# Gated linear attention with a mixture of experts: bounds and counts behind the turns, clears on ScalarE

## The chip, the cores and the metric

The program runs on one core of a Trainium2 chip. The metric is the device time of one execution in microseconds; of several executions the median is taken. The engines are called as the profile calls them: PE (TensorE; PEld is its loading of weights), DVE (VectorE), ACT (ScalarE), POOL (GpSimd) and SP (SyncE, which issues most DMAs).

## The reference

Inputs are q, k, v, a_re, a_im of shape (4, 8, 768, 48) and the weights of a gated mixture of 8 experts. First comes a linear attention whose state decays by a complex factor a of magnitude at most 0.999 (B = 4 batches, H = 8 heads, D = 48):

```python
mag = np.sqrt(a_re * a_re + a_im * a_im)
scale = np.minimum(mag, 0.999) / (mag + 1e-06)
a_re_n, a_im_n = (a_re * scale, a_im * scale)
for t in range(S):
    ar, ai = (a_re_n[:, :, t, :, None], a_im_n[:, :, t, :, None])
    new_re = ar * S_re - ai * S_im
    new_im = ar * S_im + ai * S_re
    S_re, S_im = (new_re + kv, new_im)      # kv = outer product of k and v at t
    y[:, :, t] = np.einsum('bhd,bhde->bhe', q[:, :, t], S_re)
```

Its output, as 3072 rows x of 384 numbers, goes to the experts. A row goes to the expert e with the largest logit x @ w_gate; the result is gate * sigmoid(x @ w_output_gate)[e] * (relu(x @ w1[e]) @ w2[e]), where gate is the softmax weight of e, w1[e] is 384 by 1024 and w2[e] 1024 by 384.

## The kernel before, in words

The kernel has two stages. The attention takes about the first 260 us and the experts the rest.

**Attention.** The 3072 rows are 24 chunks of 128 rows. A chunk's decays are summed along its rows by matmuls with triangular matrices: the logarithms of magnitudes give real factors, the angles give turns. Keys are multiplied by the inverse factor and queries by the factor, and both by cosine and sine of the turns, so that the recurrence becomes masked products of keys and queries inside a chunk, and a state between chunks.

Chunks are prepared in ten groups, of 1, 1, 2, 2 and then six times 3 chunks (`sizes`, numbered 0 to 9). For each group these steps run, written as Python generators so that they can be interleaved:

- `prep_exp` (L441): logarithm, exponentials and squares on ACT, products on DVE. Its last two steps are on DVE. The *bound* (L475) writes l2, the logarithm of the magnitude bounded by 0.999, which the sums of `decay` read. The *count* (L479) reads the real part ar and counts the elements that the method can take; only a check at the end of the attention reads that number. On a group of 3 chunks each is one instruction of 128x1152.
- `decay` (L493): per chunk a matmul pair (L499, tile cs), the exponentials re and ri of it on ACT (L231), k times ri (L506) and q times re (L507) on DVE.
- `turning` and `turns` (L554, L534): per chunk the angle of the chunk before is added (L530), a matmul pair sums the angles (L540, tile cs), and DVE rounds (L546), subtracts (L547, output ai) and takes the magnitude (L549, output rnd). The next chunk's turn starts from this one's. The tile cs has two PSUM buffers, which decays, turns, `ratios` (L514, which turns the rcs rows with L95) and the gates share.
- `phase` (L579): sine and cosine of the turns on ACT, into the tile trig.

Exponentials and sines need different function sets on ACT, so a group costs two set loads (L225).

`main` (L791) goes over the chunks. For chunk i it emits `turn` of chunk i+1 (L598: products with trig on DVE into kc and qc, L602; eight transposes each on PE, L95; copies kt and qt on ACT, L614), `state` (L618), `score` (L641: products sc on PE, mask on DVE, L649), `values` (L655) and `finish` (L677: transposes and the row store xn) of chunk i-1. `gates` and `chosen` (L701, L708) compute the logits of two chunks: matmuls (L242), a copy ls (L245), a transpose, and a sum (L250) that belongs to `chosen`. `routing` (L722) ranks the rows of each expert from these and enters them in a list in DRAM.

`side` (L840) is the order of a group's preparation and is stepped beside `main`. For groups after the fourth it is: load the exponential set, then `prep_exp` of the next group mixed with `decay` and `turning` of this one, then the sine set, then `phase`. `first_weights` (L930) follows the last group. It allots the experts' first buffers, among them the two tiles rows (128x1536 each) into which an expert's rows will be gathered, clears both with memsets on POOL (L947), starts the loads of the first weights (raw, L196) and splits them into a high part (L210, ACT) and a low part (L211, DVE).

**Order.** What an engine runs is not the order of this code. A scheduler lists the instructions of each engine by data dependences and a priority, which is the place in the code, moved forward by the numbers of the table `URGE` for the steps that it names (a key is a function's name, or the name with its first argument). `after(a, b, ...)` makes a come behind b in that order, without a semaphore. Every engine then runs its list strictly in order.

**Experts.** Eight experts in order of their counts; per expert the matmuls L1231 and L1169 with relu and split on ACT and DVE (L1235, L1236). Nothing in this stage is touched by the change.

## Time and profile before

| what | us |
|---|---|
| median of 3 runs | 516.22 |
| lowest and highest | 514.34, 519.79 |
| the profiled execution's own time | 514.01 |
| its span, first to last instruction | 512.2 |

The profile is of one execution. A line names the engine, the line of the kernel, output<-inputs and the shape. "Busy" is time with an instruction under way. A bracket such as [1.87 <-DVE kc L602] is the idle time of that engine before the instruction and the instruction that ended it; "issue" there means that the profile shows nothing waited for. PEclk is the granted clock of PE as a share of 2.4 GHz. In the view of instructions in order of time, equal neighbours are merged: x8 are eight instructions. Between the span and the execution's own time lie 1.8 us that no instruction fills.

### The profile page before, as it was taken

To read this page: it belongs to the slowest core of one execution; us is meant where nothing else is said; L and a number is where in the kernel's file an instruction comes from. 1 tells how busy PE (TensorE), PEld (TensorE's weight loads), DVE (VectorE), ACT (ScalarE), POOL (GpSimd) and SP (SyncE) were. 2 spreads that over 40 slices of the span, in tenths; PEclk is the share of its full clock that TensorE was granted. 3 is DMA by queue.
4 is the path that set the end of the run, shared out by engine and by line. 5 is a ranking of instruction groups with operands and counts; after the bars stand their busy time and mean duration, and the time that the engine had idled before them with its cause. 6 is when DMAs were issued, how large, how long until landed. Compare 5 with 4: busy or idle time off the path is not lost.

```text
span 512.2 us, 11231 instructions
## 1 busy us (share of the span) xinstructions
PE 485.5 (95%) x4341; PEld 425.2 (83%) x4341; DVE 338.8 (66%) x746; ACT 319.1 (62%) x605; POOL 119.0 (23%) x138
## 2 busy tenths in 40 slices
PE   7897998989999999988999999999999999999991
PEld 7575885857877877877888899999999999999991
DVE  5769999888998999996588455273644536273210
ACT  6888896978989899855734355272644536272320
POOL 4101210020402122223402732324242223020112
PEclk9999999998999999999999999999999999999996
DMA  8964344426261411007452777163361817130001
GB/s 271 301 203 136 116 117 146 127 47 203 55 176 57 105 34 33 32 21 245 136 174 74 191 180 246 48 218 124 120 187 45 283 41 237 59 92 17 21 22 47
DMA packets 46946, 63.83 MB, mean 125 GB/s; under 512 B 11815, under 2 KB 38710, under 8 KB 46884
## 3 DMA queue, kind: packets, MB, share of 16 engines
q1 hardware_dynamic: 38756, 53.61, 34.5%
q0 software_dynamic: 8128, 9.42, 6.7%
q8 instruction: 36, 0.59, 0.5%
q14 instruction: 26, 0.21, 0.1%
HBM read 53.92 MB, written 9.88 MB: 125 GB/s over the span
## 4 chain that ended last, share of the span: by engine, by line
PE 60%; issue 17%; DVE 7%; ACT 6%; DMA 4%; POOL 4%; POOLq 0%; SPq 0%; DVEq 0%; ACTq 0%
PE up L1231 12%; PE acc L1169 11%; PE tr L95 9%; PE sc L648 7%; PE xo L662 4%; PE st L627 3%; PE xo L668 3%; POOL out_dram L1182 3%; PE cs L499 3%; PE cs L540 3%; DMA ai<-in_a_im_dram 2%; ACT t L231 1%; PE tr L242 1%; DMA rows<-xd,sid 1%; PE xt L95 1%
## 5 line engine op out<-in xcount | busy, mean ns | idle before, releaser
L1236 DVE SCALAR_TENSOR_TENSOR hl<-up,hh 128x464 fp32r<-128x464 f32 (+7 forms) x64 | 37.8, 590 | 84.0 <-ACT hh L1235 80.0
L1235 ACT ACTIVATE hh<-up 128x464 fp32r<-128x464 f32 (+7 forms) x64 | 33.2, 518 | 95.0 <-PE up L1231 91.9
L1231 PE MATMUL up<-xh,w1h 128*128 128x464 f32 (+7 forms) x192 | 68.6, 357 | 0.0
L1231 PE MATMUL up<-xl,w1h 128*128 128x464 f32 (+7 forms) x192 | 67.6, 352 | 0.0
L1231 PE MATMUL up<-xh,w1l 128*128 128x464 f32 (+7 forms) x192 | 67.4, 351 | 0.0
L1169 PE MATMUL acc<-hh,w2h 128*128 128x464 f32 (+6 forms) x168 | 61.4, 365 | 0.0
L1182 POOL DMA_INDIRECT out_dram<-y,sid x28 | 31.8, 1134 | 124.9 <-ACT y L1204 121.9
L1169 PE MATMUL acc<-hh,w2l 128*128 128x464 f32 (+6 forms) x168 | 59.2, 352 | 0.0
L1169 PE MATMUL acc<-hl,w2h 128*128 128x464 f32 (+6 forms) x168 | 59.1, 354 | 0.0
L1065 POOL DMA_INDIRECT table<-entry,addr x20 | 27.8, 1388 | 131.9 <-DVE addr L1061 128.0
L648 PE MATMUL sc<-qt,kt 96*128 96x128 f32 x384 | 53.0, 281 | 0.0
L648 PEld LDWEIGHTS sc<-qt,kt 96*128 96x128 f32 x384 | 47.0, 191 | 4.5 <-issue 2.7
L1110 POOL DMA_INDIRECT rows<-xd,sid x28 | 34.7, 1239 | 51.0 <-DVE w2l L211 24.2
L662 PE MATMUL xo<-scores,v 128*48 128x128 f32 x384 | 44.4, 281 | 0.5 <-DVE scores L649 0.5
L668 PE MATMUL xo<-qt,state 96*48 96x128 f32 x320 | 37.9, 275 | 0.0
L1231 PEld LDWEIGHTS up<-xl,w1h 128*128 128x128 f32 x192 | 36.0, 188 | 1.3 <-DVE xl L1026 0.4
L211 DVE TENSOR_TENSOR w1l<-raw,w1h 128x512 fp32r<-128x512 f32 x48 | 30.4, 686 | 9.9 <-ACT w1h L210 9.9
L1231 PEld LDWEIGHTS up<-xh,w1l 128*128 128x128 f32 x192 | 36.1, 188 | 0.9
L1231 PEld LDWEIGHTS up<-xh,w1h 128*128 128x128 f32 x192 | 36.1, 188 | 0.8
L649 DVE TENSOR_TENSOR scores<-sc,mask 128x512 f32<-128x512 f32 x48 | 32.6, 683 | 5.2 <-PE sc L648 4.7
L662 PEld LDWEIGHTS xo<-scores,v 128*48 128x48 f32 x384 | 27.9, 123 | 9.8 <-issue 4.6
L1169 PEld LDWEIGHTS acc<-hh,w2h 128*128 128x128 f32 x168 | 31.6, 188 | 1.0
(211 smaller groups left out, 1090.3 us busy)
## 6 DMA issues: line engine op xcount, KB each, us to landing
raw<-in_moe_w_dram SPq DMA_DIRECT2D x32, 768.0 KB
ar<-in_a_re_dram SPq DMA_DIRECT2D x24, 192.0 KB
ai<-in_a_im_dram SPq DMA_DIRECT2D x24, 192.0 KB
k<-in_k_dram SPq DMA_DIRECT2D x24, 192.0 KB
q<-in_q_dram SPq DMA_DIRECT2D x24, 192.0 KB
v<-in_v_dram SPq DMA_DIRECT2D x24, 192.0 KB
xd<-xn SPq DMA_DIRECT2D x24, 192.0 KB
rows<-xd,sid POOLq DMA_INDIRECT x28
```

The lines of the kernel that those rows point to most:

```text
L95: return nc.tensor.transpose(out=out, in_=in_, identity=ident[p0:p0 + n, p0:p0 + n])
L211: ins = nc.vector.tensor_tensor(out=lo[:, s], in0=raw[:, s], in1=hi[:, s].bitcast(F32), op=ALU.subtract)
L648: nc.tensor.matmul(sp[:, j * P:(j + 1) * P], r["kt"][:D2, h, :], r["qt"][:D2, h, :], start=True, stop=True)
L649: nc.vector.tensor_tensor(out=r["s"][:, 4 * hh:4 * hh + 4, :], in0=sp.rearrange("p (h t) -> p h t", t=P), in1=mask[i % 2].unsqueeze(1).bro ...
L662: nc.tensor.matmul(op[u * DP:u * DP + D, j * P:(j + 1) * P], vt[c][:, h * D:(h + 1) * D], r["s"][:, h, :], start=True, stop=(cc == 0))
L668: nc.tensor.matmul(op[u * DP:u * DP + D, j * P:(j + 1) * P], xs[:D2, h * D:(h + 1) * D], r["qt"][:D2, h, :], start=False, stop=True)
L1110: nc.gpsimd.indirect_dma_start(out=rows[e % 2][:n, i, :], out_offset=None, in_=xd[:known], in_offset=bass.IndirectOffsetOnAxis(ap=ids[:n, ...
L1169: nc.tensor.matmul(accs[kt][:, :cap], w[:, cs], a, start=(ft == 0 and s == 0), stop=(ft == FT - 1 and s == 2))
L1182: ins = nc.gpsimd.indirect_dma_start(out=out, out_offset=bass.IndirectOffsetOnAxis(ap=ids(e)[:n, i:i + 1], axis=0), in_=y[:n, :], in_offse ...
L1231: nc.tensor.matmul(up[:, :cap], w[:, kt, :], x[:, kt, :], start=(m == 0), stop=(m == 3 * KT - 1))
L1235: nc.scalar.activation(out=hh, in_=up[:, :cap], func=AF.Relu)
L1236: nc.vector.scalar_tensor_tensor(out=hl, in0=up[:, :cap], scalar=0.0, in1=hh.bitcast(F32), op0=ALU.max, op1=ALU.subtract)
```

## The change

Five edits, all in the attention:

1. For groups 5 to 9, bound and count are taken out of `prep_exp` into a generator `bound`, which `side` of the group before runs after its `phase`. The bound is ordered behind the last turn (L547) of the group before. From group 4 on the count comes behind its bound; for groups 0 and 1 that was so already.
2. In `decay` the exponential ri, for the keys, is written before re, for the queries. The scheduler then also puts k times ri before q times re.
3. `URGE` has an entry of 40 for `chosen`, the sum of the gates.
4. `URGE` has an entry of 60 for `turn` of chunk 2 alone.
5. The two memsets of rows on POOL become eight multiplications of the constant iota by 0.0 on ACT, 128x384 each, emitted after the first weight loads.

```diff
@@ -405,7 +405,7 @@
             KEEPV = ()
             XTD = 0
             QTD = 0
-            URGE = {"ranked": 150, "routing": 100, ("routing", True): 300, "turning": 30, **UG}
+            URGE = {"ranked": 150, "routing": 100, ("routing", True): 300, "turning": 30, "chosen": 40, ("turn", 2): 60, **UG}
             XN = 0
             L2B = 2
             INIT = 4
@@ -471,16 +471,26 @@
                 nc.vector.scalar_tensor_tensor(out=lnr, in0=lnr, scalar=2.0, in1=t2, op0=ALU.mult, op1=ALU.add)
                 yield
                 function(out=t2, in_=lnr, func=AF.Exp, scale=-0.5, bias=b_eps)
-                d["l2"] = l2 = early.tile([P, NG, HD], F32, name="l2", bufs=L2B)
-                st["bounded"] = nc.vector.scalar_tensor_tensor(
-                    out=l2.rearrange("p c f -> p (c f)")[:, :w], in0=lnr, scalar=2.0 * math.log(0.999), in1=t2, op0=ALU.min, op1=ALU.subtract)
-                yield
-
-                ins = nc.vector.scalar_tensor_tensor(
-                    out=sq, in0=ar, scalar=0.0, in1=sq, op0=ALU.is_gt, op1=ALU.is_gt, accum_out=count[:, g:g + 1])
-                if g < 2:
-                    after(ins, st["bounded"], "bounds first")
-                yield
+
+                def bound():
+                    d["l2"] = l2 = early.tile([P, NG, HD], F32, name="l2", bufs=L2B)
+                    st["bounded"] = nc.vector.scalar_tensor_tensor(
+                        out=l2.rearrange("p c f -> p (c f)")[:, :w], in0=lnr, scalar=2.0 * math.log(0.999), in1=t2, op0=ALU.min, op1=ALU.subtract)
+                    if g > LATE:
+                        after(st["bounded"], st["turned", starts[g] - 1], "turns first")
+                    yield
+
+                    ins = nc.vector.scalar_tensor_tensor(
+                        out=sq, in0=ar, scalar=0.0, in1=sq, op0=ALU.is_gt, op1=ALU.is_gt, accum_out=count[:, g:g + 1])
+                    if not INIT > g > 1:
+                        after(ins, st["bounded"], "bounds first")
+                    yield
+
+                if g > LATE:
+                    d["bound"] = bound()
+                    yield
+                else:
+                    yield from bound()
 
             @urge
             def prep_trig(g):
@@ -501,8 +511,8 @@
                         after(st["summed"], warmed, "clock")
                     re = early.tile([P, HD], F32, name="re")
                     ri = early.tile([P, HD], F32, name="ri")
+                    function(out=ri, in_=lp[:, :HD], func=AF.Exp, scale=-1.0)
                     function(out=re, in_=lp[:, :HD], func=AF.Exp)
-                    function(out=ri, in_=lp[:, :HD], func=AF.Exp, scale=-1.0)
                     nc.vector.tensor_tensor(out=d["k"][c], in0=d["k"][c], in1=ri, op=ALU.mult)
                     nc.vector.tensor_tensor(out=d["q"][c], in0=d["q"][c], in1=re, op=ALU.mult)
                     (nc.gpsimd if g < 2 else nc.sync).dma_start(
@@ -859,6 +869,8 @@
                 if late:
                     yield from prep_trig(g)
                 yield from mix(phase(g), *([prep_trig(g + 1)] if ahead else []))
+                if ahead:
+                    yield from G[g + 1]["bound"]
                 if not more:
                     yield from ratios(g)
 
@@ -944,8 +956,11 @@
                 ready["pool"], ready["set"] = pool, weight_set(pool)
                 for n in range(2):
                     rows[n] = pool.tile([P, NS, HD], F32, name=f"rows{n}")
-                    nc.gpsimd.memset(rows[n], 0.0)
                 pieces = load_pieces(ready["stage"], who[0])
+                for n in range(2):
+                    for i in range(NS):
+                        nc.scalar.mul(rows[n][:, i, :], iota[:, :HD], 0.0)
+                    yield
                 yield from rest()
                 ready["splits"] = split_pieces(pieces, ready["set"], (st["placed"], st["listed"]))
                 for _ in range(3):
```

The counts of instructions on PE, DVE and SP stay; POOL loses two, ACT gains eight. The scheduler's lists move as follows. Line numbers are of each kernel's own file: behind the new code the same line is 10 higher (L547 is L557, L602 is L612), and L475, L479 are L477, L483.

DVE before, around the second and third turn of group 5 (the rows L546, L547, L549 are one turn; l_1559 is the bound of group 6, sq,count its count, kc and qc the next chunk's products):

```order
L547 TENSOR_TENSOR ai<-cs,rnd 128x384
L649 TENSOR_TENSOR scores<-sc,mask_88 128x512
L530 SCALAR_TENSOR_TENSOR ai<-ai,full_turn 32x384
L549 TENSOR_SCALAR rnd<-ai 128x384
L475 SCALAR_TENSOR_TENSOR l_1559<-lnr,t_1232 128x1152
L546 TENSOR_SCALAR rnd<-cs 128x384
L479 SCALAR_TENSOR_TENSOR sq,count<-ar,sq 128x1152
L547 TENSOR_TENSOR ai<-cs,rnd 128x384
L602 TENSOR_TENSOR kc_170<-k,trig 128x768
```

DVE in the changed kernel, from the same third turn on (l_1641 is the bound of group 6):

```order
L556 TENSOR_SCALAR rnd<-cs 128x384
L250 TENSOR_REDUCE logits<-cs 128x32
L557 TENSOR_TENSOR ai<-cs,rnd 128x384
L612 TENSOR_TENSOR kc_170<-k,trig 128x768
L559 TENSOR_SCALAR rnd<-ai 128x384
L659 TENSOR_TENSOR scores<-sc,mask_88 128x512
L612 TENSOR_TENSOR qc_169<-q,trig 128x768
L260 TENSOR_REDUCE mx<-logits 128x4
L477 SCALAR_TENSOR_TENSOR l_1641<-lnr,t_1280 128x1152
L262 TENSOR_TENSOR dl<-logits,mx 128x32
L483 SCALAR_TENSOR_TENSOR sq,count<-ar,sq 128x1152
```

Bound and count have left the third turn's way and stand behind the keys' and queries' products of the next chunk; the sum of the gates (L250) stands ahead of them.

ACT before, at the end of the attention (xt, state, kt and qt are copies out of PSUM, w1h the first weights' high part):

```order
L694 COPY xn<-tr 128x384
L231 ACTIVATE ex<-dl 128x32
L672 COPY xt<-xo 128x512
L231 ACTIVATE en<-los 128x4
L637 COPY state_172<-st 96x384
L614 COPY kt_174<-tr 96x512 x2
L614 COPY qt_173<-tr 96x512 x2
L210 CAST w1h_3376<-raw 128x512 x3
```

ACT in the changed kernel, same place (L962 are the clears):

```order
L231 ACTIVATE ex<-dl 128x32
L682 COPY xt<-xo 128x512
L962 ACTIVATE rows_3384<-iota 128x384 x4
L231 ACTIVATE en<-los 128x4
L962 ACTIVATE rows_3385<-iota 128x384
L647 COPY state_172<-st 96x384
L962 ACTIVATE rows_3385<-iota 128x384 x3
L624 COPY kt_174<-tr 96x512 x2
L210 CAST w1h_3376<-raw 128x512 x2
L624 COPY qt_173<-tr 96x512 x2
```

The eight clears stand between the copies xt and kt, five of them ahead of the state's copy; two of the weights' casts have moved ahead of qt.

## Rows read from the trace of the kernel before

**Rows 1.** The page's first part: busy us (share of the span) and instructions per engine.

```profile
PE 485.5 (95%) x4341; PEld 425.2 (83%) x4341; DVE 338.8 (66%) x746; ACT 319.1 (62%) x605; POOL 119.0 (23%) x138
```

**Rows 2.** By stage: length; busy us PE, PEld, DVE, ACT, POOL; PEclk, DMA share, GB/s.

```profile
60.00:210.00 150.00, 145.16 (x1807) 113.94 (x1805) 137.28 (x325) 130.01 (x237) 23.78 (x19) 0.99 0.35 96
210.00:230.00 20.00, 18.41 (x271) 15.28 (x270) 19.39 (x52) 13.74 (x28) 5.41 (x5) 1.00 0.07 22
230.00:262.00 32.00, 29.35 (x377) 25.11 (x372) 21.01 (x71) 17.55 (x37) 9.60 (x8) 1.00 0.57 174
```

**Rows 3.** Instructions of PE in order of time, 105 to 120 us: start, length; [idle before].

```profile
105.63 0.91 PE L540 MATMUL cs<-ai,tri_t 128*128 128x384 f32 x2
...
114.01 0.19 PE L95 MATMUL cs<-ident,rcs 24*96 24x24 f32 x1 [2.15 <-issue]
114.58 1.41 PE L499 MATMUL cs<-l,tri_l 128*128 128x384 f32 x2 [0.38 <-ACT rc L520]
115.78 1.92 PE L95 MATMUL tr<-ident,kc 128*96 128x128 f32 x8
...
119.31 1.08 PE L95 MATMUL tr<-ident,qc 128*96 128x128 f32 x8
```

**Rows 4.** Instructions of DVE in order of time, 109 to 121 us.

```profile
109.42 0.62 DVE L530 SCALAR_TENSOR_TENSOR ai<-ai,full_turn 32x384 f32<-32x384 f32 x1
...
110.34 1.35 DVE L475 SCALAR_TENSOR_TENSOR l<-lnr,t 128x1152 f32<-128x1152 f32 x1
...
112.08 1.35 DVE L479 SCALAR_TENSOR_TENSOR sq<-ar,sq 128x1152 f32<-128x1152 f32 x1
...
113.35 0.55 DVE L547 TENSOR_TENSOR ai<-cs,rnd 128x384 f32<-128x384 f32 x1
113.82 0.95 DVE L602 TENSOR_TENSOR kc<-k,trig 128x768 f32<-128x768 f32 x1
...
120.49 0.96 DVE L602 TENSOR_TENSOR qc<-q,trig 128x768 f32<-128x768 f32 x1 [1.86 <-PE tr L95]
```

**Rows 5.** PE by stretches of 2 us: busy, granted clock, DMA share, GB/s.

```profile
112.00:114.00 2.00, 0.00 (x0) 1.00 0.00 0
114.00:116.00 2.00, 1.61 (x5) 0.72 0.68 214
116.00:118.00 2.00, 2.00 (x12) 0.50 0.91 243
```

**Rows 6.** GpSimd (POOL), 217 to 221 us, in order of time.

```profile
217.55 2.72 POOL L947 MEMSET rows<- 128x1536 f32 x2
```

**Rows 7.** DVE, ACT and PE, 216 to 225 us, in order of time, a view each.

```profile
217.33 3.15 DVE L549 TENSOR_SCALAR rnd<-ai 128x384 int32<-128x384 int32 x1
...
224.02 0.35 DVE L549 TENSOR_SCALAR rnd<-ai 128x384 int32<-128x384 int32 x1
...
220.52 0.61 ACT L231 ACTIVATE trig<-rnd,b_cos 128x384 f32<-128x384 f32 x1 [2.75 <-DVE rnd L549]
...
221.19 0.91 PE L540 MATMUL cs<-ai,tri_t 128*128 128x384 f32 x2 [1.59 <-DVE ai L530]
```

**Rows 8.** Groups by line and shape: count | busy us, mean ns | idle before.

```profile
L694 ACT COPY xn<-tr 128x384 f32<-128x384 f32 x24 | 11.5, 480 | 4.5 <-PE tr L95 3.1 <-DVE mx L260 0.7 <-DVE q L689 0.6
```

**Rows 9.** Instructions of ACT in order of time, 230 to 237 us.

```profile
230.54 0.59 ACT L672 COPY xt<-xo 128x512 f32<-128x512 f32 x1 [0.90 <-PE xo L668]
...
232.67 0.47 ACT L637 COPY state<-st 96x384 f32<-96x384 f32 x1 [1.18 <-DVE rank L279]
233.60 1.06 ACT L614 COPY kt<-tr 96x512 f32<-96x512 f32 x2 [0.46 <-PE tr L95]
```

**Rows 10.** ACT's waits, 24 to 262 us: us in total, times, longest.

```profile
ACT trig L231 <- DVE ai L547: 4.4, 4, 1.4
```

**Rows 11.** PE and DVE, 42 to 46 us, in order of time, a view each.

```profile
44.59 1.05 PE L95 MATMUL tr<-ident,kc 128*96 128x128 f32 x8 [1.87 <-DVE kc L602]
...
43.03 0.55 DVE L506 TENSOR_TENSOR k<-k,ri 128x384 f32<-128x384 f32 x1
```

## The prediction

> **What bounds the kernel now.** I read the busy shares first, then the table by stage, then PE's own idle times in order of time, then what DVE and ACT did at each of them, and last the ends of the attention on ACT.
>
> PE has work under way for 95% of the span [rows 1]. That share hides two different halves. In the experts the change touches nothing. In the attention PE, DVE and ACT are all nearly full: from 60 to 210 us DVE is busy for 137.28 of 150 us, ACT for 130.01, PE for 145.16 [rows 2]. The PE figure is flattered, because matmuls are counted until their modelled ends. DVE has 12.72 us without work in that stretch, and that is about all that a better order can give there. From 230 us on DVE and ACT have room (21.01 and 17.55 of 32 us), and PE sets the pace [rows 2]. Whatever the attention ends earlier, the experts start earlier, as they need the last chunks before their first matmul.
>
> Two places stand out where PE stops and the instructions that the change moves are the reason.
>
> *The stop at 112 us.* PE idles 2.15 us, then 0.38 us [rows 3]. It is short of a free cs buffer and of keys: the third turn's subtraction, which frees the buffer, ends at 113.90, and the next keys' product starts only at 113.82 [rows 4]. Ahead of both stand the bound and the count of the next group, 1.35 us each [rows 4]. After the stop PE's granted clock is 0.72 and then 0.50, that is the 1.2 GHz level, where it had been 1.00 [rows 5]; the engine did nothing from 112 to 114 us before it fell. Eight transposes then take 1.92 us and a matmul pair 1.41 us, where at full clock the same forms take 1.08 and 0.91 [rows 3]. DVE works without a gap from 109.42 us until it waits 1.86 us for those slow transposes [rows 4].
>
> *The stop at 220 us.* POOL's two memsets run from 217.55 to 220.27 us [rows 6]. The small DVE operation that starts at 217.33 takes 3.15 us, where the same one takes 0.35 us six microseconds later [rows 7]. ACT waits 2.75 us for it, and PE 1.59 us for what follows it [rows 7].
>
> **The change part by part.** All terms are made against the profiled execution's own 514.01 us (512.2 us of span and 1.8 around it). It lies 2.2 us below the median of 516.22, so I add 2.2 us at the end.
>
> *Memsets off POOL.* The DVE operation shrinks from 3.15 to 0.35 us: 2.80 us of DVE, which is the upper end. PE lost 1.59 us, which is the lower end, since PE had other work until then. Between the two I take the middle, -2.2 us. The Trainium skill (SBUF — State Buffer, "Who interferes with whom") says that VectorE and GpSimd share a pair of ports, held by one of them for a whole instruction while the other is fully blocked. The rows agree: the blocked operation ended 0.2 us after the memsets. By that rule the whole 2.8 us would come back to DVE; by PE's own row only 1.59 us would reach the end.
>
> *Clears on ACT.* Eight pieces of 128x384. A copy of that shape takes 0.48 us on ACT [rows 8], the nearest row, though it reads PSUM; eight are 3.8 us. They stand between the copy xt at 230.54 and the copies kt at 233.60. ACT idles 0.90, 1.18 and 0.46 us in that stretch [rows 9], and the last two, 1.64 us, lie behind xt. So kt comes 3.8 - 1.6 = 2.2 us later if all of it is exposed, and nothing later if the earlier queries' products have already moved the queue ahead. What is queued behind: state, kt, qt, and with them PE's transposes, which need the tr buffers that kt empties; also two weight casts that now stand ahead of qt and would hold it if the weights were late. PE has gaps of its own later in that stretch, so I take +0.8 us; ends 0 and +2.2.
>
> *Bound and count behind the turns.* At the stop at 112 us the two instructions no longer stand ahead of the third turn and the keys. The most that can come back is the stop, 2.15 + 0.38 = 2.53 us, and the slow clock, (1.41 - 0.91) + (1.92 - 1.08) = 1.34 us: 3.87 us. The least is nothing: DVE must still do the same 2.7 us somewhere, and it was without a gap. What it lost for certain is its own wait of 1.86 us for slow transposes; I take -1.9 us, the value nearest to that row. At the other boundaries the same pair stands ahead of a second turn, and ACT waits 4.4 us in four places for turns, 112 us among them [rows 10]; PE did not stop there. Bounds -4.4 and, if one boundary starves as 112 us did, +3.9; I take -1.0 us. This holds the unknown effect of all the other moves too, the gates' earlier sum among them.
>
> What the delay of the bound costs: decays of the next group begin after it. The bound of group 6 ran at 110.34 and moves back past a few DVE instructions, to behind the products of the first chunk; its own keys are used only three chunks later, and 24 chunks in the 262 us of the attention are some 11 us each, an estimate from the stages [rows 2]. So nothing there. The count frees its ar buffer as much later, and SP's loads of later groups, which now stand further back in SP's queue, keep two groups' distance. I cost both at nothing.
>
> *Keys first.* It matters where the keys' product is awaited: at 44.59 us PE has idled 1.87 us for kc, and two multiplications of the second chunk (0.55 us each) stood ahead of it [rows 11]. They now stand behind, and the entry for `turn` of chunk 2 lifts the same product. At most -1.1 us; the second chunk is later by as much, so at least 0; I take -0.5 us.
>
> Sum: -2.2 + 0.8 - 1.9 - 1.0 - 0.5 = -4.8 us. 514.0 - 4.8 = 509.2 us, and with the 2.2 us to the median 511.4 us. All ends to one side give -12.2 and +4.5 us, or 504.0 and 520.7 us.
>
> **The rivals.**
>
> *DVE is the limit, the pair only changes place.* For it: DVE runs without a gap around 112 us, and 2.7 us of work remain at each boundary. Against it: DVE has 12.72 us of gaps from 60 to 210, some of them waits for PE and ACT that the stops cause. Then only DVE's own saving counts, -2.8, and the clears, +0.8: 514.2 us.
>
> *The gaps close.* For it: ACT's waits on turns at every boundary. If half of DVE's 12.72 us goes, that is -6.4 in place of the -2.9 for the bounds: -2.2 + 0.8 - 6.4 - 0.5 = -8.3, or 507.9 us. Against it: three engines above 85% busy in strict order seldom fit so well.
>
> *Slower: the stop moves on to the next chunk.* The pair now stands behind the first queries' product of a new group and ahead of the second keys' product. If PE runs dry there, the price per boundary is that of the stop at 112 us with its slow clock, 3.87 us. There are five boundaries. With one such stop the kernel stands at -2.2 + 0.8 - 0.5 + 3.9 = +2.0, or 518.2 us; with two at 522.1 us. It decides from the point where PE's stock of work is less than the 2.7 us of the pair. Against it: in the new order a mask (L659) and the first chunk's kc and qc come before the pair, and the eight transposes on each of these are 1.08 us at full clock [rows 3], some 2.2 us of stock beside the scores.
>
> *The change does not do what it says* is not a rival of weight: the lists show the pair and the memsets moved.
>
> **How the numbers follow.** The forecast has 0.50, the DVE limit 0.27, the closed gaps 0.13, the moved stop 0.10. A measurement of this kernel tells about 1% (5.2 us) from no change, so faster begins at 511.1 us and slower at 521.4 us. The forecast lies almost on the first line; I count half of its chance as faster (0.25), all of the closed gaps (0.13) and 0.02 of the DVE limit: 0.40. Slower is the moved stop with two boundaries or more, and what I cannot see: 0.07. The rest, 0.53, is within 1%. The range of 8 in 10 runs from 505.0, which holds part of the closed gaps, to 517.5, which holds the DVE limit and most of one moved stop.
>
> **What would show it.** Right: L559 never above 1 us; no PE idle above 1 us and granted clock 1.00 where group 5 turns; kc of the third group-of-three starting right behind its sine; clears of about 0.5 us each, kt waiting for no more than 2 us; the attention's last chunk 4 to 6 us earlier. Wrong: a PE idle above 2 us at another boundary with the clock at 0.50 behind it; ACT standing in a weight cast while qt is due; or DVE's gaps from 60 to 210 us still near 12.7 us, with only 2 to 3 us gained, which would be the DVE limit.

## The result and the profile after

The changed kernel takes 519.29 us (median of 12 executions, 518.35 to 523.17), the kernel before 515.57 on the same chip (12 executions, 513.59 to 519.79). The ratio is 1.0084, interval 1.0057 to 1.0111. It is slower by 0.84%, some 4 us, inside the 1% that I took as not told apart from no change, but on the other side of the forecast and above the range of 505.0 to 517.5. The profiled execution took 520.22 us, with a span of 518.4.

From the first `up` matmul of the experts to the end, the two profiles take 248.4 us (before) and 247.5 us (after). In these two profiles everything that was lost was lost in the attention: its last matmul of xo starts at 253.5 us before and at 260.7 after.

The page of the kernel after, first part (answers to [rows 1]):

```profile
PE 490.3 (95%) x4341; PEld 426.3 (82%) x4341; DVE 336.1 (65%) x746; ACT 322.5 (62%) x613; POOL 112.2 (22%) x136
```

The same engine by stage and, at the end of the attention, by 4 us (columns as in [rows 2]):

```profile
60.00:210.00 150.00, 142.03 (x1783) 111.50 (x1782) 131.25 (x308) 126.93 (x229) 19.84 (x19) 0.99 0.34 96
210.00:230.00 20.00, 19.81 (x254) 15.20 (x254) 17.08 (x47) 13.28 (x29) 2.31 (x3) 1.00 0.09 31
230.00:262.00 32.00, 29.00 (x376) 23.65 (x378) 22.81 (x76) 24.56 (x53) 9.46 (x8) 0.95 0.54 158
...
248.00:252.00 4.00, 2.21 (x13) 1.42 (x14) 3.96 (x10) 2.73 (x7) 0.00 (x0) 0.86 0.63 147
252.00:256.00 4.00, 4.00 (x38) 3.20 (x38) 1.46 (x10) 2.90 (x6) 1.07 (x1) 0.72 0.52 117
```

Against [rows 2], every engine does less from 60 to 210 us: DVE 131.25 us where it was 137.28, with 308 instructions for 325. I had hoped that DVE's gaps would close. They grew, from 12.72 to 18.75 us. The clock is not the reason, since PE's granted share is 0.99 in both.

The two stalls that I had aimed at are gone. PE of the kernel after, in order of time, where [rows 3] had the stop:

```profile
111.00 1.83 PE L658 MATMUL sc<-qt,kt 96*128 96x128 f32 x14
113.46 0.91 PE L550 MATMUL cs<-ai,tri_t 128*128 128x384 f32 x2 [0.63 <-DVE ai L540]
...
116.55 1.08 PE L95 MATMUL tr<-ident,kc 128*96 128x128 f32 x8 [0.68 <-DVE kc L612]
...
249.79 0.64 PE L95 MATMUL tr<-ident,kc 128*96 128x128 f32 x4 [2.40 <-ACT xn L704]
```

The stop of 2.15 us at 112 us is gone, and what is left are waits of 0.63 and 0.68 us. But one of the signs that I had named for being wrong is there too, one boundary earlier. PE of the kernel after, and the stretch behind it (columns as in [rows 2]):

```profile
83.50 1.57 PE L550 MATMUL cs<-ai,tri_t 128*128 128x384 f32 x2 [2.01 <-DVE ai L540]
84.00:86.00 2.00, 2.00 (x8) 1.22 (x7) 1.34 (x3) 0.04 (x1) 0.00 (x0) 0.50 0.22 48
```

PE idles 2.01 us and its granted clock is 0.50 behind that. In the profile before, the idle time at this place is 1.43 us. It is 2.0 to 2.1 us in every profile with all of edit 1, and 0.9 to 1.4 us in all others.

The small DVE operation that the memsets had held for 3.15 us [rows 7], in the group by tile rnd, 205 to 232 us (count of instructions, min/median/max ns, first and last start):

```profile
L559 DVE TENSOR_SCALAR rnd<-ai x2: 353/355/357, 216.5 to 228.2; 128x384 int32<-128x384 int32 x2
```

This stall went, but not by edit 5 alone. Run k2 is the changed kernel with the memsets left on POOL. There they run in order of time, beside a DVE product, as

```profile
223.13 2.73 POOL L959 MEMSET rows<- 128x1536 f32 x2
225.10 0.96 DVE L612 TENSOR_TENSOR kc<-k,trig 128x768 f32<-128x768 f32 x1 [2.05 <-ACT trig L231]
```

and the small operation is at its ordinary length from 205 to 240 us:

```profile
L559 DVE TENSOR_SCALAR rnd<-ai x3: 338/350/353, 216.7 to 232.3; 128x384 int32<-128x384 int32 x3
```

With the other edits in, the bound's move among them, it no longer falls beside the memsets (in e2, the move alone, it still does in part and takes 1.70 us), and the product that does takes the same 0.96 us as elsewhere. So here the memsets held nothing that edit 5 could give back.

The clears and what follows them, ACT of the kernel after in order of time (answers to [rows 9]):

```profile
235.99 0.57 ACT L682 COPY xt<-xo 128x512 f32<-128x512 f32 x1
236.46 1.76 ACT L962 ACTIVATE rows<-iota 128x384 f32<-128x384 f32 x4
...
238.22 0.51 ACT L962 ACTIVATE rows<-iota 128x384 f32<-128x384 f32 x1
...
238.99 1.35 ACT L962 ACTIVATE rows<-iota 128x384 f32<-128x384 f32 x3
240.25 1.05 ACT L624 COPY kt<-tr 96x512 f32<-96x512 f32 x2
...
249.25 0.48 ACT L704 COPY xn<-tr 128x384 f32<-128x384 f32 x1 [3.03 <-DVE q L699]
```

The eight clears are 1.76 + 0.51 + 1.35 = 3.6 us, as costed (3.8), and ACT has no gap around them. kt starts 4.26 us behind xt; in k2, without clears, 2.13 us. So the clears hold kt back by 2.1 us, my upper end of 2.2. Ten microseconds later PE stops for 2.40 us for xn (its row above), ACT having waited 3.03 us for DVE. There DVE was late too, in order of time:

```profile
247.00 0.56 DVE L646 TENSOR_TENSOR st<-st,rc 96x384 f32<-96x384 f32 x1 [3.49 <-PE sc L658]
...
248.67 0.55 DVE L699 TENSOR_TENSOR q<-tr,k 128x384 fp32r<-128x384 f32 x1
```

PE's last product for st (L637) had ended at 244.61; DVE starts 2.4 us after it and 0.2 us after PE has worked off the scores that follow (246.81). This lateness is told in the last section. The clock falls behind the stop, to 0.86 and 0.72 in the stretches of 4 us above.

### The profile page after: what moved, and what is told of

Read it like the earlier page. It is cut to its first block, busy times and chain, and to the rows that moved or that the text cites. A ratio compares the mean times of both kernels' runs of the same rounds, so it can differ in the third digit from the quotient of the medians.

```text
span 518.4 us, 11246 instructions
## 1 busy us (share of the span) xinstructions
PE 490.3 (95%) x4341; PEld 426.3 (82%) x4341; DVE 336.1 (65%) x746; ACT 322.5 (62%) x613; POOL 112.2 (22%) x136
## 4 chain that ended last, share of the span: by engine, by line
PE 65%; issue 16%; DVE 6%; ACT 6%; POOL 3%; DMA 1%; POOLq 0%; SPq 0%; DVEq 0%; ACTq 0%
PE up L1246 12%; PE acc L1184 12%; PE tr L95 10%; PE sc L658 7%; PE xo L672 4%; PE xo L678 4%; PE cs L550 3%; PE st L637 3%; POOL out_dram L1197 3%; PE cs L509 3%; PE tr L242 1%; PE xt L95 1%; PE yp L95 1%; ACT t L231 1%; PE tr L902 1%
## 5 line engine op out<-in xcount | busy, mean ns | idle before, releaser
L1080 POOL DMA_INDIRECT table<-entry,addr x20 | 24.5, 1224 | 131.7 <-DVE addr L1076 114.1
L678 PE MATMUL xo<-qt,state 96*48 96x128 f32 x320 | 40.5, 276 | 0.0
L659 DVE TENSOR_TENSOR scores<-sc,mask 128x512 f32<-128x512 f32 x48 | 32.8, 684 | 8.2 <-PE sc L658 7.9
L95 PE MATMUL tr<-ident,kc 128*96 128x128 f32 x192 | 27.7, 287 | 6.2 <-DVE kc L612 3.6
```

The costliest lines, as they stand in the source:

```text
L95: return nc.tensor.transpose(out=out, in_=in_, identity=ident[p0:p0 + n, p0:p0 + n])
L659: nc.vector.tensor_tensor(out=r["s"][:, 4 * hh:4 * hh + 4, :], in0=sp.rearrange("p (h t) -> p h t", t=P), in1=mask[i % 2].unsqueeze(1).bro ...
L678: nc.tensor.matmul(op[u * DP:u * DP + D, j * P:(j + 1) * P], xs[:D2, h * D:(h + 1) * D], r["qt"][:D2, h, :], start=False, stop=True)
```

## The experiments

Ratios are to the kernel before, timed on the same chip, with the 95% interval; 12 executions each where nothing else is said. Four chips were used: one for the runs e, a second for f, a third for a, g, h and k, a fourth for p. All kernels compute everything. The diffs show the lines that tell a run from its neighbours, not whole edits.

### Each edit alone, and each taken out

Edit 5 alone, 1 alone, 3 alone, 2 alone, in this order:

```diff
# e1_clears: only
-                    nc.gpsimd.memset(rows[n], 0.0)
+                        nc.scalar.mul(rows[n][:, i, :], iota[:, :HD], 0.0)
# e2_bound: only
+                    yield from G[g + 1]["bound"]
# e4_chosen: only
+ "chosen": 40
# e3_keys: only ri ahead of re
```

> The kernel before with edit 5 alone: the rows are cleared by eight ACT multiplications, not by two POOL memsets. Theory A (the moved bound costs the time) and theory B (the gates' earlier sum costs it) expect the same here: the 3.15 us DVE operation beside the memsets shrinks to 0.35 us, the eight clears cost ACT some 3.4 us where it has room, and the time is 1 to 2 us below before (513.5 to 514.5 against 515.6 us). Theory C (the clears hold ACT at the end of the attention, where the changed kernel's PE idles 2.40 us at 249.79 us and its clock falls) expects 2 to 4 us above before.

> The kernel before with edit 1 alone: bound and count of groups 5 to 9 behind the turns of the group before. Theory A (the moved bound lets DVE reach the next group late, and DVE then waits for PE): 4 to 7 us above before, some 520 to 522 us, with keys' products 8 to 13 us later from the third group of three on, and DVE waiting 5 us or more for turns' sums. Theory B (the gates' sum): no more than 1 us from before, or 2 us below, as the stop at 112 us goes. Theory C (the clears): 2 us below.

> The kernel before with edit 3 alone: the gates' sum has a priority of 40. Theory B (the sum stands ahead of keys' products on DVE and waits there for PE's logits, so the strictly ordered DVE stands still): 3 to 5 us above before, 519 to 521 us. Theory A (the moved bound) and theory C (the clears): within 1 us of before, 514.6 to 516.6 us.

> The kernel before with edit 2 alone: ri and k times ri ahead of re and q times re. My forecast's term was -0.5 us (0 to -1.1): 514.5 to 515.6 us. Theories A, B and C all expect no loss here; if it is 2 us or more above before, the order of keys and queries is itself the cause, as queries' factors come late in every group.

Measured: clears 1.0036 (1.0005 to 1.0067); bound 1.0011 (0.9979 to 1.0043); gates' sum 0.9999 (0.9965 to 1.0033); keys 0.9995 (0.9961 to 1.0029). Only the clears show anything, and that a loss, near the lower end of what theory C asked for (0.36% is some 1.9 us). Theory A is not met by e2, nor B by e4. None of the four alone makes the 0.84%; edit 4 alone was not run.

Then the changed kernel with one edit undone: 1, 3, 5 and 4.

```diff
# f2_nobound: bound and count back in prep_exp
-                    yield from G[g + 1]["bound"]
# f4_nochosen
- "chosen": 40
# f1_noclears
+                    nc.gpsimd.memset(rows[n], 0.0)
-                        nc.scalar.mul(rows[n][:, i, :], iota[:, :HD], 0.0)
# f5_noturn2
- ("turn", 2): 60
```

> The changed kernel with edit 1 undone (bound and count where they were), the four other edits kept. Alone, edits 1, 2, 3 and 5 moved the kernel by no more than 2 us, so the 4 to 5 us of the whole lie in edits that act together, or in edit 4. Theory D (the moved bound and the gates' earlier sum together: both put DVE work that waits for PE ahead of the next keys' products): 513 to 515.5 us, the loss is gone. Theory E (edit 4, the entry for the turn of chunk 2) and theory F (keys first together with the rest): 518 us or more, as here.

> The changed kernel with edit 3 undone (no entry for the gates' sum), the four other edits kept. Theory D (moved bound and gates' sum together): 514 to 516.5 us, and keys' products no more than some 5 us later than before. If only the moved bound matters beside the clears: 518 us or more. Theory E (edit 4): 518 us or more.

> The changed kernel with edit 5 undone (memsets on POOL again). The chunk's second mask in the changed kernel is already 2.0 us late at 217 us, before the clears run, and 4.8 us late at 246 us. Theory D: 517 to 519.5 us, within 2 us of the changed kernel. Theory C (clears at the end of the attention, with the fall of PE's clock at 250 us): 514.5 to 516 us.

> The changed kernel with edit 4 undone (no entry for the turn of chunk 2). It moves four instructions on DVE and seven on PE near 45 us. Theory D: 518.5 to 520 us, the loss stays. Theory E (edit 4 starts a delay near 45 us that lasts): 514 to 516 us.

Measured: without the bound's move 0.9956 (0.9927 to 0.9986), now faster than before; without the gates' entry 1.0055 (1.0023 to 1.0086); without the clears 0.9992 (0.9956 to 1.0028); without the entry for chunk 2 1.0093 (1.0052 to 1.0135, 8 executions). The loss goes with the bound or with the clears, and stays without edits 3 or 4. Theory D is met by f5 and, in kind, by f2, and missed by f1 and f4; E is not met.

### Which of the two, and in what company

Edits 2 to 4 alone; the clears written earlier, where the memsets stood; and the changed kernel twice more on this chip.

```diff
# g2_keys_gates: edits 2, 3, 4 only
# g1_early: in the changed kernel
                     rows[n] = pool.tile([P, NS, HD], F32, name=f"rows{n}")
+                    for i in range(NS):
+                        nc.scalar.mul(rows[n][:, i, :], iota[:, :HD], 0.0)
                 pieces = load_pieces(ready["stage"], who[0])
```

> The changed kernel once more, for a second profile of the same program. Up to its ACT clears at 236 us it runs the same lists as the run without clears, and yet in the first profile it was 5.6 us behind that run by 228 us, 1.3 of them from a fall of PE's clock at 22 us. Theory G (chance: this lag is of the execution, not of the program): the lag by 228 us is within 2 us here, and the loss comes behind 236 us. Theory H (the lag belongs to the program): 4 to 6 us again.

> As the run before, a third profile of the changed kernel. Theory G expects a lag by 228 us that differs from the first profile's 5.6 us by 2 us or more; theory H 4 to 6 us again.

> The changed kernel with the eight clears still on ACT but emitted at the place of the old memsets, ahead of the first weight loads, so that they stand in two blocks of four ahead of the state's copy, and the copies kt, the casts and the state products behind them stand otherwise. Theory I (not the clears' 3.6 us, but the order that the scheduler makes around them costs: DVE then waits 3.49 us for the state's products and holds the splits behind it): 514 to 516 us. Theory C (the clears' own time on ACT): 518 us or more, as before the edit.

> The kernel before with edits 2, 3 and 4 alone: keys first, the gates' sum and the turn of chunk 2 earlier, with the memsets on POOL and the bound where it was. With the clears beside them these edits gave 512.5 us against 513.9 of before. If the clears gain about 2 us where the bound is not moved (the forecast's memset term): 514 to 515 us here. If the clears cost there too, as they did alone (515.6 against 514.5 us): 510.5 to 512 us.

Measured: edits 2 to 4 alone 0.9945 (0.9914 to 0.9977). Early clears 1.0031 (0.9994 to 1.0067), an interval that touches no change; their 516.90 us lies between theories I and C, so their place wasn't settled. The two single executions of the changed kernel, a1 and a2, took 523.66 and 519.47 us; what parts them is in the last section. By 228 us both lie 4.5 us behind f1 (second mask of the chunk, with the first masks set equal), as theory H had it. But k2, which is f1's own program on this chip, lies 4.6 us behind it: the lag is not of the clears, and goes with the chip.

With edits 2 to 4 in, there are now four cases: neither other edit 0.9945, clears only 0.9956 (f2), bound only 0.9992 (f1), both 1.0084 (after). They come from different chips, so two of them were timed again on the chip of g2, beside two variants of the bound.

```diff
# k1_after: the changed kernel; k2_noclears: f1 again
# h1_count: edits 2 to 4; the bound stays, the count alone goes behind the turns
+                    if g > LATE:
+                        after(ins, st["turned", starts[g] - 1], "turns first")
# h2_six: edits 2 to 4; edit 1 for group 6 only
-                    if g > LATE:
+                    if g == 6:
```

> The changed kernel, timed beside the next three on one chip. Theory J (the moved bound and the ACT clears cost together): 518.5 to 520.5 us, and 4 us or more above the same kernel without clears. Theory K (chance and chips: the two were timed on different chips): within 2 us of it.

> The changed kernel with edit 5 undone, once more, on the chip of the run before. Theory J: 513.5 to 515.5 us. Theory K: 518 us or more where the changed kernel stands at 519 to 520. If PE's signals come late here too (as they did in the profiles of the kernel before and the changed one, by 1 to 2.5 us at some ten places, and in no profile of this kernel so far), the lateness belongs to the chip and not to the program.

> Edits 2, 3 and 4, and of edit 1 the count alone: the count of groups 5 to 9 goes behind the turns, the bound stays where it was; memsets on POOL. With no part of edit 1 this stood at 512.5 us (0.55% below before). Theory L (the delay of the bound, on which the next group's sums wait, is what edit 1 costs): the count alone costs nothing and the stop at 112 us shrinks, 511 to 512.5 us. Theory M (any 1.35 us instruction behind the turns pushes keys' products back): 513.5 us or more.

> Edits 2, 3 and 4, and edit 1 for group 6 alone, whose bound stood ahead of the turn in the stop at 112 us; memsets on POOL. If the gain at the stop is real and the later boundaries give it back: 510.5 to 512 us, and the chunks behind 115 us 2 us or more earlier than with no part of edit 1. If the loss follows from one moved pair alone: 513.5 us or more.

Measured: both 1.0067 (1.0031 to 1.0102); bound only 1.0036 (1.0001 to 1.0072); the count alone 0.9959 (0.9921 to 0.9996); one group 1.0001 (0.9970 to 1.0033). So on one chip 0.9945 goes to 1.0036 by the move of the bound, and to 1.0067 by the clears on top. On this chip the move of the bound is the larger part, 0.91%, with intervals that do not meet, and the clears 0.31%, which alone would be within the intervals. On f1's chip the shares lie the other way: f1, with the move and no clears, is at 0.9992, and f5, with both and without edit 4, at 1.0093. k1 stands where theory J had it; k2's 516.92 us lies between J and K. h2 is in the range of a loss from one moved pair alone.

Where the bound costs it is read from g2 and k1. Start of the second mask on DVE (L649, L659) in nine of the chunks, us:

```
g2      101.64 115.37 124.67 140.88 160.27 177.79 194.86 213.38 249.58
k1      101.58 113.72 122.22 143.01 161.08 182.50 200.37 218.88 255.57
k1-g2    -0.06  -1.65  -2.45  +2.13  +0.81  +4.71  +5.51  +5.50  +5.99
```

The changed kernel gains 2.45 us by 125 us, where the stop was, and gives back 4.6 us by 141 and, after a small gain, 3.9 more by 178. The first clear runs at 233 us, so the +5.50 at 213 us is without any. The experts' first matmul follows: 262.16 in g2, 267.88 in k1.

The same is seen on f1's chip. Up to 217 us f1 and f2 differ in edit 1 alone:

```
f2      102.03 115.54 126.47 142.69 162.07 179.43 196.50 215.02
f1      103.25 114.49 122.98 141.66 159.83 180.76 197.96 216.56
f1-f2    +1.22  -1.05  -3.49  -1.03  -2.24  +1.33  +1.46  +1.54
```

The gain at the stop is given back here too, and more: 5.0 us from 125 to 216 us, against 8.0 us from g2 to k1. (In these two profiles f1 has lost some 1.2 us to a slow clock at 82 to 86 us and f2 some 1.6 us at 115 to 120.)

Why: the bounds of the five groups and the keys' products, by line, 60 to 230 us. First g2 (count of instructions, min/median/max ns, first and last start):

```profile
L475 DVE SCALAR_TENSOR_TENSOR l<-lnr,t x5: 1334/1357/1368, 75.3 to 188.1; 128x1152 f32<-128x1152 f32 x5
...
L602 DVE TENSOR_TENSOR kc<-k,trig x19: 925/951/959, 63.0 to 229.3; 128x768 f32<-128x768 f32 x19
```

and k1:

```profile
L477 DVE SCALAR_TENSOR_TENSOR l<-lnr,t x5: 1344/1347/1349, 88.7 to 202.2; 128x1152 f32<-128x1152 f32 x5
...
L612 DVE TENSOR_TENSOR kc<-k,trig x17: 945/948/959, 63.1 to 221.9; 128x768 f32<-128x768 f32 x17
```

The first bound runs 13.4 us later, the last 14.1 (some 5 us of this last are the lag that k1 has by then), and by 230 us DVE has made two keys' products fewer. How the delay comes about is seen where the next bound, of group 7, stands. DVE of g2 in order of time:

```profile
134.26 1.36 DVE L475 SCALAR_TENSOR_TENSOR l<-lnr,t 128x1152 f32<-128x1152 f32 x1 [0.24 <-ACT t L231]
135.54 0.55 DVE L546 TENSOR_SCALAR rnd<-cs 128x384 f32<-128x384 f32 x1
...
140.41 0.56 DVE L546 TENSOR_SCALAR rnd<-cs 128x384 f32<-128x384 f32 x1
```

and of k1:

```profile
140.83 0.55 DVE L556 TENSOR_SCALAR rnd<-cs 128x384 f32<-128x384 f32 x1
141.67 0.96 DVE L612 TENSOR_TENSOR kc<-k,trig 128x768 f32<-128x768 f32 x1 [0.30 <-ACT trig L231]
...
143.88 0.95 DVE L612 TENSOR_TENSOR qc<-q,trig 128x768 f32<-128x768 f32 x1
144.75 1.35 DVE L477 SCALAR_TENSOR_TENSOR l<-lnr,t 128x1152 f32<-128x1152 f32 x1
146.09 1.35 DVE L483 SCALAR_TENSOR_TENSOR sq<-ar,sq 128x1152 f32<-128x1152 f32 x1
...
149.40 0.95 DVE L612 TENSOR_TENSOR kc<-k,trig 128x768 f32<-128x768 f32 x1
```

Here the bound stood ahead of two turns, not one, and now waits for both and for the products of the next chunk; the pair itself stands ahead of the second chunk's keys. The keys of the second chunk start at 149.40, where g2 has them at 144.01; those of the third chunks of groups 6, 7 and 8 start 8.3, 9.5 and 13.3 us later (146.55 to 154.82, 173.82 to 183.30, 200.66 to 213.92). In g2 they ran 9 to 12 us ahead of the first mask of the chunk before; in k1 2 to 7. DVE had lost its stock of work and waits, by its waits of 60 to 230 us (us in total, times, longest). First g2:

```profile
DVE kc L602 <- ACT trig L231: 1.9, 3, 0.7
DVE rnd L546 <- PE cs L540: 1.7, 4, 0.6
DVE scores L649 <- PE sc L648: 1.4, 4, 0.5
```

and k1:

```profile
DVE rnd L556 <- PE cs L550: 5.5, 4, 2.0
DVE scores L659 <- PE sc L658: 4.9, 6, 2.4
DVE kc L612 <- ACT trig L231: 3.3, 4, 2.1
```

The three sum to 5.0 and 13.7 us; on f1's chip to 6.5 in f2 and 12.6 in f1. The 2.4 us among them, at 140 us, is in part of another kind, told in the last section: in f1 the same mask waits 0.6 us.

h1 takes the rival that any work put behind the turns costs as much. It moves half of the pair, the count, and its profile ends the attention 0.6 us ahead of g2 (last xo 256.05 against 251.70, less a start that was 4.94 us later). If each half cost the same, 0.9990 was due; 0.9959 was measured, and 0.9990 lies just inside the interval. Its 514.47 us lies in the range of theory M; its distance of 0.14% from g2 speaks for L. In its profile the stop at 112 us is gone too; its masks are 1.4 us ahead of g2's at 115 us and 2.0 us behind at 195 (starts set equal). So a count behind the turns gives back some of its gain as well, and whether the late bound or the displaced products cost the time was not separated. h2 shows the exchange at one boundary: its profile gains 5 us against g2 by 115 us and has lost it and 3.5 us more by 150, with a new stop and a slow clock behind it. One moved pair costs 0.56% against g2, more than half of what five cost. PE of h2 by stretches of 4 us:

```profile
144.00:148.00 4.00, 2.31 (x11) 1.27 (x11) 4.00 (x7) 3.66 (x8) 0.00 (x0) 0.91 0.36 65
148.00:152.00 4.00, 4.00 (x34) 2.77 (x32) 3.43 (x8) 1.88 (x4) 0.00 (x0) 0.66 0.09 30
```

### What starts the experts

The best variant, g2, and the changed kernel, each with the fourth load of first weights behind the loads of the routing's lists on SP.

```diff
-                pieces = load_pieces(ready["stage"], who[0])
+                pieces = load_pieces(ready["stage"], who[0], 0, 3)
                 yield from rest()
+                pieces += load_pieces(ready["stage"], who[0], 3)
```

> Edits 2, 3 and 4 (512.5 us, 0.55% below before) with the fourth of the first weights' loads put behind the loads of the lists on SP. Theory N (the experts start 17.1 us after the first list has become row numbers on DVE, sid, in every profile of that chip; the list waits for the scatters into the table, and these land late beside the 0.75 MB weight load): sid 2 to 4 us earlier, 1 to 3 us less in time, 509.5 to 511.5 us, as then the last chunk sets the start. Theory O (the end of the attention on PE sets the experts' start, as the forecast had it): within 1 us of 512.5, or slower, as the late load holds ACT's casts.

> The whole change, with the fourth weight load behind the loads of the lists. In its profiles this load went out at 248.2 us, just ahead of the lists at 248.8, and sid came 4.9 us after the lists went out, where it takes 1.6 to 2.0 us without such a load beside it. Theory N: sid 3 us earlier or more, 515.5 to 517.5 us, so that about half of the 4 us of loss at the seam is this collision. Theory O: 519 us as before.

Measured: 0.9935 (0.9904 to 0.9966) and 1.0072 (1.0035 to 1.0108). The list's numbers came about 2.4 us sooner than in g2 and k1 (starts set equal), the experts' first matmul at most 0.8 us. In these profiles it follows the last xo by 10 to 10.5 us, as in before and after: the last chunk on PE sets it there, not the chain of the lists, and theory O is met. (The 17.1 us of the expectation are 18.5 in k2.) p1, 512.18 us, has the lowest ratio of all; against g2 the 0.1% is not told apart.

That holds for twelve of the profiles. In the eight of the chips of e and f the first matmul follows the last xo by 12.1 to 16.0 us, and PE waits 1.3 to 3.1 us for gathered rows; in none of the twelve does it wait for them. PE of f5:

```profile
261.80 3.40 PE L1030 MATMUL sc<-ident,rows 116*128 116x116 f32 x14 [3.09 <-DMA rows<-xd,sid]
```

There the gathered rows set the start, and part of what edits cost is paid at them: f5's last xo is 0.7 us behind f1's (starts set equal), its first matmul of the experts 3.2 us. The later weight load was not run on those chips.

## Why the prediction was wrong

*The delay of the bound: the step that failed.* I wrote that the bound "moves back past a few DVE instructions" and that "its own keys are used only three chunks later", and costed the delay at nothing. I had read it at one boundary, 112 us, where it stood ahead of one turn and moves by 4.8 us (110.5 in g2, 115.3 in k1). At the other four it stood further ahead and moves by 10.5 to 14 us. Three chunks later was true of the first use, but the keys of the third chunks lost 4 to 7 us of the 9 to 12 that they had been ahead. "Other boundaries", -1.0, became some +8 on the chip of g2 and k1 (from -2.45 at 125 us to +5.50 at 213) and +5 on f1's. That the move costs is shown by g2 and k2; that it does so through the lost lead of DVE fits the rows, but the late bound and the pair's own 2.7 us were not told apart.

*The rival "the stop moves on to the next chunk"* (chance 0.10) comes nearest, and its number by luck: 3.87 us forecast per boundary, 4.6 and 3.9 measured at the two that cost most, and +3.7 us for the whole, between one such boundary (+2.0) and two (+5.9). Its price was a stop of PE with the clock at 0.50 behind it. At a boundary such a stop came only at 83 us, in the profile after; k1, with the same stop and its clock at 1.00, had lost nothing to g2 by 102. At the dear boundaries PE of k1 idles at most 1.07 us, the granted clock is 1.00 from 125 to 220 us, and about 2 us of the 4.6 are the lateness of the last section.

*The stop at 112 us*: it went, and the size is right, -2.45 against -1.9. The term was luck: I had taken DVE's wait for slow transposes, and in g2, whose clock stayed at 1.00 there, that wait does not exist. How the 2.45 us divide was not shown.

*Memsets off POOL and clears on ACT*: the stall went (3.15 to 0.36 us), but -2.2 + 0.8 became a loss: +0.36% alone, +0.1% without the bound's move (f2 against g2, two chips), +0.31% with it (k1 against k2). Here I added two terms, the move of the bound and the memsets, that remove the same stall. Without the move, the 1.59 us of PE did come back: between the same two masks, at some 197 and 225 us, e3 (with memsets) takes 28.4 us and e1 (with clears) 26.8. Why e1 is still slower was not shown; against e3 its profile shows no loss behind 195 us. With the move and edits 2 to 4 there was no stall left to take away (k1 and k2 both take 29.7 us between these masks), and the clears, which met no idle ACT as at my upper end of +2.2, were all cost. The stop of 2.40 us is in five profiles with both edits (after, a1, a2, k1, p2), and in all five DVE starts the state product 2.3 to 2.4 us after PE has ended it. In f5, with both edits (but not edit 4) on f1's chip, DVE starts 0.1 us after, and PE has no stop above 0.9 us there; nor has g1, with the clears earlier. So the lateness has its part in that stop; how the two edits lead up to it wasn't shown.

*Keys first and the gates' sum*: each alone nothing (-0.5 forecast). Together with edit 4 they give -0.55%, if the bound stays. Which of them carries it wasn't separated, and the parts were timed on another chip than g2. I had put the gates' earlier sum into the unknown effect of "all the other moves"; alone it has none.

By the steps on one chip: -0.55% (edits 2 to 4), +0.91% (bound), +0.31% (clears) make +0.67%, some 3.5 us; I had -0.9% in all.

## What to carry to other kernels

An instruction that starts a later group's preparation is not idle baggage in front of a stall: ask at each boundary where it goes, and what the engine would have worked ahead with. Before two gains are added, ask whether one edit already removes what the other is to remove: here the moved bound took the DVE operation away from the memsets. A stop that is taken away at one place is worth its length only if the lead of the engines behind it stays, so follow a chunk's start to the end of the stage before a gain is counted. And an edit's worth hangs on the others and on the chip: the parts alone, on one chip, gave nothing or little; on another all five gave +0.67%, and three of them without the rest -0.55%.

## What the runs showed of the hardware

**The same program waits at other places on another chip.** f1 and k2 are one program, 0.9992 on one chip and 1.0036 on the other. ACT of f1 in order of time:

```profile
136.90 1.28 ACT L225 ACT_TABLE_LOAD   x1
138.19 0.58 ACT L682 COPY xt<-xo 128x512 f32<-128x512 f32 x1
```

PE of f1:

```profile
137.60 0.48 PE L678 MATMUL xo<-qt,state 96*48 96x128 f32 x3
```

ACT of k2:

```profile
137.70 1.28 ACT L225 ACT_TABLE_LOAD   x1
141.65 0.59 ACT L682 COPY xt<-xo 128x512 f32<-128x512 f32 x1 [2.67 <-PE sc L658]
```

PE of k2:

```profile
138.39 0.48 PE L678 MATMUL xo<-qt,state 96*48 96x128 f32 x3
...
140.45 1.05 PE L658 MATMUL sc<-qt,kt 96*128 96x128 f32 x8
142.53 0.43 PE L672 MATMUL xo<-scores,v 128*48 128x128 f32 x4 [1.03 <-ACT xt L682]
```

In f1 the copy xt starts 0.1 us after the last xo ends (138.08). In k2 it starts 2.8 us after (138.87), when PE has worked off its scores, and PE then waits for it. The same 2.7 to 2.8 us stand there in the profiles of k1, after, a1, a2, g1 and p2, and at most 0.3 in the other profiles with the move on the chips of e and f (f4, f5, e2). Between f1 and k2 the masks after the scores at 112, 144 and 250 us and the xt at 201 (times of k2) are later behind their matmuls by 0.9 to 2.4 us too. The cause stays open. It makes the bound's move dearer in the profiles: k2 falls from 0.1 us ahead of f1 at 103 us to 5.5 us behind at 216, of which some 1.6 are a slow clock at 144 to 148 us in k2. g2 and f2, without the move, stay within 1.3 us of each other over the same stretch, f2 behind by its slow clock; g2 falls back only behind 232 us, where one xt is 2.6 us late. From g2 to k2 on one chip the move cost 0.91%; on the other f1, which has the move but not the clears, is 0.36% above f2, which has the clears but not the move. In the measured times this is not told apart, as the intervals of f1 and k2 overlap.

**The clock falls at the start in some executions and not in others.** PE of a1 by stretches of 4 us (columns as in [rows 2]):

```profile
22.00:26.00 4.00, 4.00 (x12) 2.12 (x10) 2.51 (x5) 1.20 (x2) 0.00 (x0) 0.50 1.02 338
26.00:30.00 4.00, 4.00 (x21) 2.55 (x21) 1.92 (x4) 2.26 (x5) 0.00 (x0) 0.50 0.42 147
```

and of a2, the same program on the same chip:

```profile
22.00:26.00 4.00, 4.00 (x30) 2.67 (x30) 3.46 (x8) 2.99 (x7) 0.00 (x0) 1.00 1.02 355
26.00:30.00 4.00, 4.00 (x49) 1.75 (x48) 3.54 (x7) 2.43 (x5) 0.00 (x0) 1.00 0.82 260
```

At 1.2 GHz for 8 us a1 falls 4.7 us behind a2 by its first mask and ends 4.2 us behind (523.66 and 519.47 us). Five of the twenty profiles start as late as a1, those of a1, e2, h1, h2 and p1, so two profiles are only compared after their start has been set equal; of after's 6.2 us more span than before, some 1.4 are of this kind.

**The same stop does not always cost the clock.** The 2.15 us at 112 us stand in six more profiles, all without the bound's move; behind them the granted share falls to 0.50 in before, e1, e4, f2 and p1 (there the stop ends at 118.8 us, and the 0.50 stands at 121 to 123), and stays at 1.00 in e3 and g2. The 1.34 us that I charged for it in the upper end are there in some executions only.
